# A fused Fourier-mixing and squared-ReLU kernel: chunks of 512 pairs instead of 256, 512-wide first-layer matmuls, one square for two steps, DFT matmuls in runs of three

## The chip, the cores and the metric

The kernel runs on one core of one Trainium2 chip. The metric is the device time of one execution in microseconds (us), median of several. The profile's span, from the first to the last instruction, is about 1.8 us shorter than the time of the same execution. A run counts as *fast* here if it lies within 1.5% of the fastest of its kernel. Engines in the profile are PE (TensorE, matmul), PEld (its weight loads), DVE (VectorE), ACT (ScalarE), POOL (GpSimd) and SP (SyncE).

## The reference

```python
# x: (8, 3008, 256) * 0.1;  w_in: (256, 2048);  w_out: (2048, 256)
X = np.fft.fft(np.fft.fft(x, axis=1), axis=2).real      # per batch
h = np.maximum(X.reshape(24064, 256) @ w_in, 0.0)
out = (h * h) @ w_out
```

The kernel folds the DFT over the model dimension into the first-layer weights (matrices G1, G2, G3) and does the DFT over the sequence as matmuls with cosine and sine tables on half of the frequencies. Frequency k and its mirror S-k form a *pair*: 1505 pairs per batch, 12040 in all. The hidden layer is computed for a *chunk* of pairs at a time. For an f-block of 128 hidden features, G1*P + G2*Q gives one member of the pair, and adding G3*Q to the same PSUM tile turns it into the other member. Each is sent through ReLU (ACT), squared (DVE) and used as stationary weights of the second layer.

## The kernel before

The parts that the change and the argument touch (cuts marked `# ...`):

```python
CH = 256                      # pairs in a chunk: 47 chunks of 256 and one of 8
psx = ctx.enter_context(tc.tile_pool(name="psx", bufs=3, space=PSUM))   # first layer, tables
pso = ctx.enter_context(tc.tile_pool(name="pso", bufs=2, space=PSUM))   # second layer
psf = ctx.enter_context(tc.tile_pool(name="psf", bufs=3, space=PSUM))   # DFT

def x_front(c, fp):           # one step: two f-blocks of one chunk
    # ...
    xb = psx.tile([P, 2, CH], F32, name="xb", tag="x")
    for j in range(2):
        fs = slice((fp * 2 + j) * P, (fp * 2 + j + 1) * P)
        for sn, G in ((0, G1), (1, G2)):
            for (b, i, o, l) in segs:           # two segments where a batch ends in the chunk
                mm(xb[:, j, o : o + l], G[:, fs], PQ[b][sn][:, i : i + l], first, sn == 1)
    # ...
    act(r[:, 0, :, 0:n], xb[:, :, 0:n], AF.Relu)

def x_back(cur):
    # ... the G3 matmuls into the same xb
    act(r[:, 1, :, 0:n], xb[:, :, 0:n], AF.Relu)
    vt(h2[:, 0, :, 0:n], r[:, 0, :, 0:n], r[:, 0, :, 0:n], op=ALU.mult)
    rr = r[:, 1, :, n - 1 :: -1]                # the mirror member, read in reverse
    vt(h2[:, 1, :, 0:n], rr, rr, op=ALU.mult)

for si, (c, fp) in enumerate(steps):
    take = [mmq.pop(0) for _ in range(min(len(mmq), 8))]   # second-layer matmuls, chunk before
    cur = x_front(c, fp)
    posts = [f() for f in take[:4]]
    if prev is not None:
        x_back(prev)
    posts += [f() for f in take[4:]]
    # ... evictions and stores of finished output tiles
    # ... mm2_ops of the chunk before join mmq when its last step is squared
    for f in side.get(si, []):                  # the next batch's fold (DVE) and DFT (PE, one
        f()                                     # matmul at a time), tables, weight casts
```

For each engine this is the order of its instructions. The second layer's matmuls are called `po` in the profile, the first layer's `xb`, the DFT's `pf`; `h` is the squared tile, `r` the ReLU output.

## Time and profile before

| | before |
|---|---|
| time, median of 3 runs | 658.08 us (657.77 to 658.36) |
| PE busy, share of the span of 657.9 us in the profiled execution | 635.4 us, 97% |
| ACT, DVE busy | 519.3 us, 403.3 us |
| matmuls po / xb / pf | 3040 / 2640 / 240 |
| granted TensorE clock | 1.0 |

These are lines of the page of the kernel before: busy time of each engine, the granted clock of PE in 40 equal slices of the span (9 is 90% or more), and the chain of waits that ended last, by engine and by engine, tile and line.

```profile
PE 635.4 (97%) x5954; PEld 550.0 (84%) x5954; DVE 403.3 (61%) x1078; ACT 519.3 (79%) x934; POOL 50.9 (8%) x66
...
PEclk9999999999999999999999999999999999999999
...
PE 94%; DVE 3%; DMA 1%; POOL 1%; ACT 1%; issue 0%; POOLq 0%; DVEq 0%
PE po L74 50%; PE xb L74 37%; PE pf L74 6%; DMA wst<-in_moe_w_in_dram 1%; POOL x L102 0%; DVE h L546 0%; DVE h L544 0%; DVE wout L603 0%; DVE tm L250 0%; ACT r L532 0%; ACT win L294 0%; PE ps L74 0%; DVE tt L246 0%; DVE v L334 0%; DVE tt L185 0%
```

The chain is PE almost throughout, so time is lost or won on PE. "Busy" alone does not tell whether PE is at its peak, since matmuls overlap in the record (272 ns long on average, 109 ns from start to start).

The page's groups of instructions: line, engine, operation, out<-in with shapes, count | busy us, mean ns of one | idle time before them and what ended most of it.

```profile
L74 PE MATMUL po<-wout,h 128*128 128x256 f16 (+1 forms) x3040 | 452.8, 272 | 0.0
L74 PE MATMUL xb<-qt,G 128*128 128x256 f16 (+8 forms) x1760 | 332.3, 257 | 3.3 <-ACT r L532 2.6
...
L546 DVE TENSOR_TENSOR h<-r 128x512 f16<-128x512 f16 (+1 forms) x384 | 160.6, 418 | 239.8 <-ACT r L542 239.1
L532 ACT ACTIVATE r<-xb 128x512 f16<-128x512 f32 (+1 forms) x384 | 226.5, 590 | 98.0 <-PE xb L74 86.1
```

One step in the steady state, from the timeline of the kernel before (start us, duration us, engine, line, operation, count; in brackets idle time before it and who ended it):

```profile
310.18 0.27 PE L74 MATMUL xb<-pt,G 128*128 128x256 f16 x1
310.29 0.27 PE L74 MATMUL xb<-qt,G 128*128 128x256 f16 x1
310.40 0.27 PE L74 MATMUL xb<-pt,G 128*128 128x256 f16 x1
310.51 0.27 PE L74 MATMUL xb<-qt,G 128*128 128x256 f16 x1
...
310.62 0.60 PE L74 MATMUL po<-wout,h 128*128 128x256 f16 x4
...
311.05 0.38 PE L74 MATMUL xb<-qt,G 128*128 128x256 f16 x2
...
311.06 0.42 DVE L544 TENSOR_TENSOR h<-r 128x512 f16<-128x512 f16 x1
...
311.27 0.60 PE L74 MATMUL po<-wout,h 128*128 128x256 f16 x4
311.47 0.60 ACT L542 ACTIVATE r<-xb 128x512 f16<-128x512 f32 x1
...
311.71 0.32 PE L74 MATMUL pf<-sinT,w 127*127 127x376 f16 x1
```

The durations, 0.27 us for a 256-wide matmul, are not what one costs: the starts are 0.11 us apart. From here on a matmul's cost is the distance from its start to the next one's start, taken from the matmul records. In this trace the median is 109 ns for the 256-wide po and 215 to 216 for the 512-wide matmuls (pc, ps). The line through 109 and 215.5 is 0.416 ns for each column plus 2.5 ns for each matmul. Sums below take 0.4167 ns and 2.5 ns. The 256-wide xb are at 110.

### The profile page before, as it was taken

What the parts mean: (1) busy time and instruction counts of PE and PEld (TensorE: products, weight loads), DVE (VectorE), ACT (ScalarE), POOL (GpSimd) and SP (SyncE); (2) the same over time, 40 slices, a digit from 0 to 9 for tenths busy, and PEclk for the clock granted to TensorE, in tenths of its full rate; (3) what the DMA queues carried; (4) which work ended last, traced back from release to release, by engine and by line L of the source; (5) the groups of instructions that cost most, each with busy time, mean ns of one, the idle gap of its engine ahead of it and who ended that gap; (6) DMA issues with size and microseconds to landing.
All of it is one profiled execution on the core that took longest, in us unless ns stands there. A gap on an engine that the chain in (4) does not pass through costs nothing.

```text
span 657.9 us, 14937 instructions
## 1 busy us (share of the span) xinstructions
PE 635.4 (97%) x5954; PEld 550.0 (84%) x5954; DVE 403.3 (61%) x1078; ACT 519.3 (79%) x934; POOL 50.9 (8%) x66
## 2 busy tenths in 40 slices
PE   3779999999999999999999999999999999999998
PEld 1458889888788889888898887988899888998886
DVE  7899559779587554865568555455545555454451
ACT  5787777877778888887888787888788888888883
POOL 7203003113020000400000000000000000000000
PEclk9999999999999999999999999999999999999999
DMA  8947218276355111721111111111111111111111
GB/s 244 291 116 188 67 35 225 77 207 168 102 132 142 35 38 43 202 70 50 33 49 34 50 40 43 33 45 40 47 35 50 37 46 41 41 45 45 42 49 50
DMA packets 33772, 54.65 MB, mean 83 GB/s; under 512 B 4446, under 2 KB 28562, under 8 KB 33702
## 3 DMA queue, kind: packets, MB, share of 16 engines
q0 software_dynamic: 6256, 27.45, 16.1%
q1 hardware_dynamic: 27398, 26.22, 12.8%
q8 instruction: 46, 0.75, 0.5%
q14 instruction: 24, 0.20, 0.1%
q10 hardware_dynamic: 48, 0.02, 0.0%
HBM read 29.02 MB, written 24.64 MB: 82 GB/s over the span
## 4 chain that ended last, share of the span: by engine, by line
PE 94%; DVE 3%; DMA 1%; POOL 1%; ACT 1%; issue 0%; POOLq 0%; DVEq 0%
PE po L74 50%; PE xb L74 37%; PE pf L74 6%; DMA wst<-in_moe_w_in_dram 1%; POOL x L102 0%; DVE h L546 0%; DVE h L544 0%; DVE wout L603 0%; DVE tm L250 0%; ACT r L532 0%; ACT win L294 0%; PE ps L74 0%; DVE tt L246 0%; DVE v L334 0%; DVE tt L185 0%
## 5 line engine op out<-in xcount | busy, mean ns | idle before, releaser
L74 PE MATMUL po<-wout,h 128*128 128x256 f16 (+1 forms) x3040 | 452.8, 272 | 0.0
L74 PE MATMUL xb<-qt,G 128*128 128x256 f16 (+8 forms) x1760 | 332.3, 257 | 3.3 <-ACT r L532 2.6
L74 PEld LDWEIGHTS <-h 128*128 128x128 f16 (+1 forms) x3040 | 289.9, 97 | 33.5 <-issue 0.2
L546 DVE TENSOR_TENSOR h<-r 128x512 f16<-128x512 f16 (+1 forms) x384 | 160.6, 418 | 239.8 <-ACT r L542 239.1
L532 ACT ACTIVATE r<-xb 128x512 f16<-128x512 f32 (+1 forms) x384 | 226.5, 590 | 98.0 <-PE xb L74 86.1
L74 PEld LDWEIGHTS <-G 128*128 128x128 f16 x2640 | 237.8, 97 | 44.9 <-issue 10.2
L542 ACT ACTIVATE r<-xb 128x512 f16<-128x512 f32 (+1 forms) x384 | 226.2, 589 | 20.4 <-PE xb L74 2.3
L74 PE MATMUL xb<-pt,G 128*128 128x256 f16 (+8 forms) x880 | 187.8, 257 | 0.7 <-ACT G L304 0.3
L544 DVE TENSOR_TENSOR h<-r 128x512 f16<-128x512 f16 (+1 forms) x384 | 158.1, 412 | 0.0
L476 ACT ACTIVATE os<-po 128x512 f32<-128x512 f32 (+1 forms) x95 | 56.3, 593 | 4.0 <-PE po L74 4.0
L326 DVE TENSOR_TENSOR u<-x 127x765 f16<-127x765 f32 x32 | 29.0, 948 | 2.4 <-DMA x<-in_x_dram,idx 2.4
L74 PE MATMUL pf<-cosT,w 127*128 127x377 f16 (+1 forms) x96 | 28.9, 325 | 0.4 <-DVE cosT L281 0.4
L74 PE MATMUL pf<-sinT,w 127*127 127x377 f16 (+1 forms) x96 | 28.9, 325 | 0.0
L102 POOL DMA_INDIRECT x<-in_x_dram,idx x18 | 26.6, 1478 | 5.4 <-issue 5.1
L74 PEld LDWEIGHTS <-w 127*128 127x128 f16 (+1 forms) x192 | 22.5, 118 | 3.0 <-DVE w L339 0.2
L125 POOL DMA_DIRECT2D x<-in_x_dram x14 | 7.8, 560 | 217.0 <-DVE u L330 217.0
L339 DVE TENSOR_TENSOR w<-v 127x381 f16<-127x381 f16 x64 | 20.4, 351 | 0.0
L334 DVE TENSOR_TENSOR v<-u 127x768 f16<-127x768 f16 x32 | 16.8, 548 | 0.0
L74 PEld LDWEIGHTS <-ez 127*128 127x128 f16 (+1 forms) x42 | 4.4, 107 | 14.7 <-DVE ez L565 10.9
L381 ACT ACTIVATE as<-pf 128x377 f32<-128x377 f32 (+5 forms) x32 | 15.5, 486 | 1.4 <-PE pf L74 1.1
L74 PE MATMUL warm<-ez 128*128 128x512 f16 x18 | 5.8, 484 | 10.9 <-DVE ez L565 10.9
L417 DVE TENSOR_TENSOR pt<-pf,as 128x377 f16<-128x377 f32 (+1 forms) x16 | 8.8, 547 | 0.3
(94 smaller groups left out, 122.6 us busy)
## 6 DMA issues: line engine op xcount, KB each, us to landing
out_dram<-os SPq DMA_DIRECT2D x157, 128.0 KB
x<-in_x_dram POOLq DMA_DIRECT2D x14, 756.0 KB
wst<-in_moe_w_in_dram POOLq DMA_DIRECT2D x4, 512.0 KB, 8.9
wot<-in_moe_w_out_dram POOLq DMA_DIRECT2D x1, 2048.0 KB, 18.8
x<-in_x_dram SPq DMA_DIRECT2D x2, 756.0 KB
x<-in_x_dram,idx POOLq DMA_INDIRECT x18, 11.2
x<-in_x_dram POOLq DMA_DIRECT2D x14, 2.0 KB, 10.8
out_dram<-os SPq DMA_DIRECT2D x2, 108.0 KB
```

The lines of the kernel that those rows point to most:

```text
L74: nc.tensor.matmul(o, l, r, start=start, stop=stop, skip_group_check=True)
L102: nc.gpsimd.indirect_dma_start(out=x4[0:NP, 2 + s, q : q + rows, :].rearrange("p q d -> p (q d)"), out_offset=None, in_=bass.AP(tensor=x.t ...
L326: return lambda: vt(u[k, s, q0 : q0 + NQ // 2, 1:D], x4[k, s, q0 : q0 + NQ // 2, 1:D], x4[k, 3 - s, ::-1, :][:, q0 : q0 + NQ // 2, D - 1 : ...
L334: return lambda: vt(v[k, s, qs, :], u[k, 0, qs, :], u[k, 1, qs, :], op=ALU.subtract if s else ALU.add)
L339: return lambda: vt(w[k, i, q : q + 3, 0 : P - 1], v[k, s, q : q + 3, 1:P], v[k, s, q : q + 3, D - 1 : P : -1], op=ALU.add if i < 2 else A ...
L381: act(st["a"][0:m, :], st[0][0:m, :], AF.Copy, bias=0.0, scale=1.0) \
L417: vt(hi_, bp, a, op=ALU.subtract)
L476: act(os_[0:m], st["o"][0:m], AF.Copy, bias=0.0, scale=HS * HS)
L532: act(r[:, 0, :, 0:n], xb[:, :, 0:n], AF.Relu)
L542: act(r[:, 1, :, 0:n], xb[:, :, 0:n], AF.Relu)
L544: vt(h2[:, 0, :, 0:n], r[:, 0, :, 0:n], r[:, 0, :, 0:n], op=ALU.mult)
L546: vt(h2[:, 1, :, 0:n], rr, rr, op=ALU.mult)
```

## The change

Its intent: fewer and wider first-layer matmuls (with a chunk of 512 pairs one f-block fills the 128 x 512 PSUM tile that two f-blocks of 256 shared), half of the weight loads of that layer, far fewer DVE instructions, and no chunk of 8 pairs at the end. The first two chunks stay at 256 pairs with two f-blocks per step. The diff, cut to its core:

```diff
-    NF = NFC // 2
-    CH = 256
+    CH = 512
-    osp = ctx.enter_context(tc.tile_pool(name="osp", bufs=4))
-    psx = ctx.enter_context(tc.tile_pool(name="psx", bufs=3, space=PSUM))
+    osp = ctx.enter_context(tc.tile_pool(name="osp", bufs=3))
+    psx = ctx.enter_context(tc.tile_pool(name="psx", bufs=6, space=PSUM))
-    psf = ctx.enter_context(tc.tile_pool(name="psf", bufs=3, space=PSUM))
 ... (SBUF space found: win16, v and the table temporaries share buffers)
-    def dft_ops(blk, mms, m, fin):            # one matmul per call
+    def dft_ops(blk, mms, m, fin, run=3):     # three matmuls per call; PSUM from psx
 ...
+    sizes = [CH // 2, CH // 2]
+    while sum(sizes) < NPAIR:
+        sizes.append(min(CH, NPAIR - sum(sizes)))     # 256, 256, 22 x 512, 264
 ...
+        groups = [tiles[i : i + 2] for i in range(0, len(tiles), 2)]
+        if n > full:                                  # the last 8 pairs: both members
+            groups.insert(0, [(2, full, n - full)])   # in one 16-wide weight tile
 ...
-        act(r[:, 1, :, 0:n], xb[:, :, 0:n], AF.Relu)
+        act(r_of(c, u, 1)[:, :, ::-1], xb, AF.Relu)   # ACT writes in reverse
 ...
+    def x_square(cur):
+        if u % 2 == 0:
+            return
+        # one multiply for two steps: 2048 elements per partition
+        vt(h2, r, r, op=ALU.mult)
 ...
-    FOLD = {0: [(1, 0.35, 0.52)], ...
-    ST1 = {0: (0.55, 0.95), 1: (0.25, 0.85)}
+    FOLD = {0: [(1, 0.5, 0.66)], ...
+    ST1 = {0: (0.66, 0.98)}                           # others 0.38 to 0.86
 ...
-        take = [mmq.pop(0) for _ in range(min(len(mmq), 8))]
+        left = NFC // chunks[c][2] - u
+        take = [mmq.pop(0) for _ in range(-(-len(mmq) // left))]
```

More of the change, by code (lines that the diff above doesn't have):

```diff
@@ L134 @@
     idx2 = iota("idx2", [P, 1], [[0, 1]], NQ // 2 * (NP - 1), -NQ // 2, I32)
-    win16 = const.tile([P, 2, F], F16, name="win16")
     wout16 = const.tile([P, NFC, D], F16, name="wout16")
@@ L235, in nk @@
                 if h == 0:
-                    tb["t"] = tgp.tile([P, NQ, HG], F32, name="tt", tag=f"tt{blk}")
-                    tb["m"] = tgp.tile([P, NQ, HG], F32, name="tm", tag=f"tm{blk}")
+                    tb["t"] = tgp.tile([P, NQ, HG], F32, name="tt", tag="tt")
+                    tb["m"] = tgp.tile([P, NQ, HG], F32, name="tm", tag="tm")
                 vt(views()[1], nval[:, qs].unsqueeze(2).to_broadcast([P, hq, ng]), kb, op=ALU.mult)
@@ L290, with win16 @@
     G3 = const.tile([P, F], F16, name="G3")
+    winh = {}
+    def win16(c):
+        if c // 2 not in winh:
+            winh[c // 2] = bfp.tile([P, 2, 1024], F16, name="win16", tag="w")
+        return winh[c // 2][:, :, c % 2 * 512 : c % 2 * 512 + 512]
     def gcast(c, cp):
-        cs = slice(c * 512, (c + 1) * 512)
-        cp(win16[:, :, cs], wst[:, :, cs])
+        cp(win16(c), wst[:, :, c * 512 : (c + 1) * 512])
     def gmat(c):
@@ L299, in gmat @@
         for t in range(2):
-            mm(pc, cosD[:, t, :], win16[:, t, cs], t == 0, t == 1)
+            mm(pc, cosD[:, t, :], win16(c)[:, t, :], t == 0, t == 1)
         ps = psx.tile([P, 512], F32, name="ps", tag="x")
         for t in range(2):
-            mm(ps, sinD[:, t, :], win16[:, t, cs], t == 0, t == 1)
+            mm(ps, sinD[:, t, :], win16(c)[:, t, :], t == 0, t == 1)
         act(G1[:, cs], pc, AF.Copy, bias=0.0, scale=1.0 / HS)
@@ L319, in fold_ops @@
         u = uvp.tile([P, 2, NQ, D], F16, name="u", tag="u")
-        v = uvp.tile([P, 2, NQ, D], F16, name="v", tag="v")
+        vs = {}
         w = bfp.tile([P, 4, NQ, P], F16, name="w", tag="w")
@@ L333, in half, with f @@
             qs = slice(h * NQ // 2, (h + 1) * NQ // 2)
-            return lambda: vt(v[k, s, qs, :], u[k, 0, qs, :], u[k, 1, qs, :],
-                              op=ALU.subtract if s else ALU.add)
+            def f():
+                if h == 0:
+                    vs[s] = uvp.tile([P, NQ, D], F16, name="v", tag="v")
+                vt(vs[s][k, qs, :], u[k, 0, qs, :], u[k, 1, qs, :],
+                   op=ALU.subtract if s else ALU.add)
+            return f
         def feat(i, q):
             s = i % 2
-            return lambda: vt(w[k, i, q : q + 3, 0 : P - 1], v[k, s, q : q + 3, 1:P],
-                              v[k, s, q : q + 3, D - 1 : P : -1],
+            return lambda: vt(w[k, i, q : q + 3, 0 : P - 1], vs[s][k, q : q + 3, 1:P],
+                              vs[s][k, q : q + 3, D - 1 : P : -1],
                               op=ALU.add if i < 2 else ALU.subtract)
@@ L344, in f @@
             def f():
-                nc.vector.tensor_copy(w[k, s, :, P - 1], v[k, s, :, 0])
+                nc.vector.tensor_copy(w[k, s, :, P - 1], vs[s][k, :, 0])
                 if b in INL:
-                    nc.vector.tensor_copy(ez[k, s, :, P - 1], v[k, s, :, P])
+                    nc.vector.tensor_copy(ez[k, s, :, P - 1], vs[s][k, :, P])
                 else:
-                    nc.vector.tensor_copy(eall[k, s, :, b], v[k, s, :, P])
+                    nc.vector.tensor_copy(eall[k, s, :, b], vs[s][k, :, P])
             return f
@@ L370, in dft_ops, with some, stage1_ops @@
         ops = []
-        def one(par, i):
+        def some(par, lo, hi):
             def f():
-                if i == 0:
-                    st[par] = psf.tile([P, HE], F32, name="pf", tag="pf")[:, 0:n]
-                hi, wt, q, tab = mms(par)[i]
-                mm(st[par][0:hi, :], wt(q), tab[k, q, c0 : c0 + n], i == 0, i == len(mms(par)) - 1)
-                if i == len(mms(par)) - 1:
-                    if par == 0:
-                        st["a"] = asp.tile([P, HE], F32, name="as", tag="as")[:, 0:n]
-                        act(st["a"][0:m, :], st[0][0:m, :], AF.Copy, bias=0.0, scale=1.0) \
-                            if fin[0] is None else act(st["a"][0:m, :], st[0][0:m, :], AF.Copy,
-                                                       bias=0.0, scale=fin[0])
-                    else:
-                        fin[1](st["a"][0:m, :], st[1][0:m, :])
+                ms = mms(par)
+                if lo == 0:
+                    st[par] = psx.tile([P, 512], F32, name="pf", tag="x")[:, 0:n]
+                for i in range(lo, hi):
+                    rows, wt, q, tab = ms[i]
+                    mm(st[par][0:rows, :], wt(q), tab[k, q, c0 : c0 + n], i == 0,
+                       i == len(ms) - 1)
+                if hi < len(ms):
+                    return
+                if par == 0:
+                    st["a"] = asp.tile([P, HE], F32, name="as", tag="as")[:, 0:n]
+                    act(st["a"][0:m, :], st[0][0:m, :], AF.Copy, bias=0.0,
+                        scale=1.0 if fin[0] is None else fin[0])
+                else:
+                    fin[1](st["a"][0:m, :], st[1][0:m, :])
             return f
         for par in range(2):
-            ops += [one(par, i) for i in range(len(mms(par)))]
+            nm = len(mms(par))
+            ops += [some(par, i, min(i + run, nm)) for i in range(0, nm, run)]
         return ops
-    def stage1_ops(b, blk, inline_e=False):
+    def stage1_ops(b, blk, inline_e=False, run=3):
         def lists(sn):
@@ L422, in stage1_ops @@
             ops += dft_ops(blk, lists(sn), P - 1 if sn and not inline_e else P,
-                           (sgn[:, 0:1] if sn and inline_e else None, fin(sn)))
+                           (sgn[:, 0:1] if sn and inline_e else None, fin(sn)), run)
         return ops
@@ L452 @@
     NPAIR = B * NK
+    sizes = [CH // 2, CH // 2]
+    while sum(sizes) < NPAIR:
+        sizes.append(min(CH, NPAIR - sum(sizes)))
+    assert all(n <= CH // 2 or n == CH or n % P < P // 4 for n in sizes)
     chunks = []
-    for g in range(0, NPAIR, CH):
-        n = min(CH, NPAIR - g)
+    g = 0
+    for n in sizes:
         segs = []
@@ L462, with h2v @@
             o += l
-        chunks.append((g, n, segs))
+        chunks.append((g, n, CH // n, segs))
+        g += n
     h2t = {}
+    def h2v(c):
+        n = chunks[c][1]
+        return h2t[c][:, 0 : NFC * 2 * n].rearrange("p (f t) -> p f t", f=NFC)
     def mm2_ops(c):
-        g0, n, segs = chunks[c]
-        tiles = [(s, t0, min(P, n - t0)) for s in range(2) for t0 in range(0, n, P)]
+        g0, n, nf, segs = chunks[c]
+        full = n // P * P
+        tiles = [(s, t0, P) for s in range(2) for t0 in range(0, full, P)]
+        groups = [tiles[i : i + 2] for i in range(0, len(tiles), 2)]
+        if n > full:
+            groups.insert(0, [(2, full, n - full)])
@@ L470, in mm2_ops @@
         ops = []
         st = {}
-        def store(grp):
-            os_ = osp.tile([P, 2, D], F32, name="os", tag="os")
-            m = max(t[2] for t in grp)
-            act(os_[0:m], st["o"][0:m], AF.Copy, bias=0.0, scale=HS * HS)
-            for j, (s, t0, m) in enumerate(grp):
-                o = 0
-                base = g0 + n - t0 - m if s else g0 + t0
-                while o < m:
-                    b, i = divmod(base + o, NK)
-                    if i < NE:
-                        l = min(m - o, NE - i)
-                        kk = 2 * i
-                    else:
-                        l = min(m - o, NK - i)
-                        kk = 2 * (i - NE) + 1
-                    lo, hi = 0, l
-                    if s and kk == 0:
-                        lo = 1
-                    if s and kk + 2 * (l - 1) == M:
-                        hi = l - 1
-                    if hi > lo:
-                        if s:
-                            r0 = b * S + S - (kk + 2 * (hi - 1))
-                            p0 = m - (o + hi)
-                        else:
-                            r0 = b * S + kk + 2 * lo
-                            p0 = o + lo
-                        nl = hi - lo
-                        nc.sync.dma_start(out=out[r0 : r0 + 2 * nl - 1 : 2, :],
-                                          in_=os_[p0 : p0 + nl, j, :])
-                    o += l
@@ L505, in one, with rows_out @@
-        def one(ti, fc):
-            s, t0, m = tiles[ti]
+        def rows_out(s, t0, m, src):
+            base = g0 + n - t0 - m if s else g0 + t0
+            o = 0
+            while o < m:
+                b, i = divmod(base + o, NK)
+                if i < NE:
+                    l = min(m - o, NE - i)
+                    kk = 2 * i
+                else:
+                    l = min(m - o, NK - i)
+                    kk = 2 * (i - NE) + 1
+                lo, hi = 0, l
+                if s and kk == 0:
+                    lo = 1
+                if s and kk + 2 * (l - 1) == M:
+                    hi = l - 1
+                if hi > lo:
+                    if s:
+                        r0 = b * S + S - (kk + 2 * (hi - 1))
+                        p0 = m - (o + hi)
+                    else:
+                        r0 = b * S + kk + 2 * lo
+                        p0 = o + lo
+                    nl = hi - lo
+                    nc.sync.dma_start(out=out[r0 : r0 + 2 * nl - 1 : 2, :], in_=src(p0, nl))
+                o += l
@@ new lines, in store @@
+        def store(grp, po):
+            os_ = osp.tile([P, 2, D], F32, name="os", tag="os")
+            if grp[0][0] == 2:
+                _, t0, m = grp[0]
+                act(os_[0 : 2 * m, 0], po[0 : 2 * m, 0], AF.Copy, bias=0.0, scale=HS * HS)
+                rows_out(0, t0, m, lambda p0, nl: os_[p0 : p0 + nl, 0, :])
+                rows_out(1, t0, m, lambda p0, nl: os_[m + p0 : m + p0 + nl, 0, :])
+                return
+            act(os_, po, AF.Copy, bias=0.0, scale=HS * HS)
+            for j, (s, t0, m) in enumerate(grp):
+                rows_out(s, t0, m, lambda p0, nl, j=j: os_[p0 : p0 + nl, j, :])
@@ L508, in f, with one @@
+        def one(grp, j, fc):
+            s, t0, m = grp[j]
             def f():
-                if ti % 2 == 0 and fc == 0:
+                if j == 0 and fc == 0:
                     st["o"] = pso.tile([P, 2, D], F32, name="po", tag="po")
-                mm(st["o"][0:m, ti % 2, :], h2t[c][:, s, fc, t0 : t0 + m], wout16[:, fc, :],
-                   fc == 0 and ti % 2 == 0, fc == NFC - 1)
-                if fc == NFC - 1 and ti % 2 == 1:
-                    return lambda: store(tiles[ti - 1 : ti + 1])
@@ L515, in one @@
-            return f
-        return [one(ti, fc) for ti in range(len(tiles)) for fc in range(NFC)]
-    def x_front(c, fp):
-        g0, n, segs = chunks[c]
-        if fp == 0:
-            h2t[c] = h2p.tile([P, 2, NFC, CH], F16, name="h2", tag="h2")
-        xb = psx.tile([P, 2, CH], F32, name="xb", tag="x")
-        first = True
-        for j in range(2):
-            fs = slice((fp * 2 + j) * P, (fp * 2 + j + 1) * P)
+                o = n + n % P + t0 if s == 1 else t0
+                w = 2 * m if s == 2 else m
@@ new lines, in f, with r_of @@
+                mm(st["o"][0:w, j, :], h2v(c)[:, fc, o : o + w], wout16[:, fc, :],
+                   fc == 0 and j == 0, fc == NFC - 1)
+                if fc == NFC - 1 and j == len(grp) - 1:
+                    return lambda o=st["o"]: store(grp, o)
+            return f
+        for grp in groups:
+            ops += [one(grp, j, fc) for j in range(len(grp)) for fc in range(NFC)]
+        return ops
+    rt = {}
+    def r_of(c, u, s):
+        g0, n, nf, segs = chunks[c]
+        if u % 2 == 0 and s == 0:
+            t = rp.tile([P, 4 * CH], F16, name="r", tag="r")
+            rt[c, u // 2] = t[:, 0 : 4 * nf * n].rearrange("p (f s n) -> p f s n", f=2 * nf, s=2)
+        o = u % 2 * nf
+        return rt[c, u // 2][:, o : o + nf, s, :]
@@ L527, in x_front @@
+    def x_front(c, u):
+        g0, n, nf, segs = chunks[c]
+        xb = psx.tile([P, 512], F32, name="xb", tag="x")[:, 0 : nf * n] \
+            .rearrange("p (f n) -> p f n", f=nf)
+        for j in range(nf):
+            fs = slice((u * nf + j) * P, (u * nf + j + 1) * P)
             for sn, G in ((0, G1), (1, G2)):
                 for (b, i, o, l) in segs:
-                    mm(xb[:, j, o : o + l], G[:, fs], PQ[b][sn][:, i : i + l], first, sn == 1)
-                    first = False
-        r = rp.tile([P, 2, 2, CH], F16, name="r", tag="r")
@@ L532, in x_front @@
-        act(r[:, 0, :, 0:n], xb[:, :, 0:n], AF.Relu)
-        return (c, fp, xb, r)
+                    mm(xb[:, j, o : o + l], G[:, fs], PQ[b][sn][:, i : i + l],
+                       j == 0 and sn == 0 and o == 0, sn == 1)
+        act(r_of(c, u, 0), xb, AF.Relu)
+        return (c, u, xb)
     def x_back(cur):
-        c, fp, xb, r = cur
-        g0, n, segs = chunks[c]
-        for j in range(2):
-            fs = slice((fp * 2 + j) * P, (fp * 2 + j + 1) * P)
+        c, u, xb = cur
+        g0, n, nf, segs = chunks[c]
@@ L540, in x_back @@
+        for j in range(nf):
+            fs = slice((u * nf + j) * P, (u * nf + j + 1) * P)
             for (b, i, o, l) in segs:
                 mm(xb[:, j, o : o + l], G3[:, fs], PQ[b][1][:, i : i + l], False, True)
-        act(r[:, 1, :, 0:n], xb[:, :, 0:n], AF.Relu)
-        h2 = h2t[c][:, :, 2 * fp : 2 * fp + 2, :]
-        vt(h2[:, 0, :, 0:n], r[:, 0, :, 0:n], r[:, 0, :, 0:n], op=ALU.mult)
-        rr = r[:, 1, :, n - 1 :: -1]
-        vt(h2[:, 1, :, 0:n], rr, rr, op=ALU.mult)
+        act(r_of(c, u, 1)[:, :, ::-1], xb, AF.Relu)
@@ new lines, in x_square @@
+    def x_square(cur):
+        c, u, _ = cur
+        nf = chunks[c][2]
+        if u % 2 == 0:
+            return
+        if u == 1:
+            h2t[c] = h2p.tile([P, NFC * 2 * CH], F16, name="h2", tag="h2")
+        r = rt.pop((c, u // 2))
+        n = chunks[c][1]
+        h2 = h2v(c)[:, (u - 1) * nf : (u + 1) * nf]
+        if n % P == 0:
+            h2 = h2.rearrange("p f (s n) -> p f s n", s=2)
+            vt(h2, r, r, op=ALU.mult)
+            return
+        full = n // P * P
+        for s, i, l, o in ((0, 0, n, 0), (1, full, n - full, n), (1, 0, full, 2 * n - full)):
+            vt(h2[:, :, o : o + l], r[:, :, s, i : i + l], r[:, :, s, i : i + l], op=ALU.mult)
@@ L580 @@
     gcast(2, nc.vector.tensor_copy)
-    s1 = stage1_ops(0, 0, True)
+    s1 = stage1_ops(0, 0, True, 1)
     for i in (0, 1, 3, 2, *range(4, len(s1))):
@@ L585 @@
     gcast(3, nc.vector.tensor_copy)
-    steps = [(c, fp) for c in range(len(chunks)) for fp in range(NF)]
+    steps = [(c, u) for c, ch in enumerate(chunks) for u in range(NFC // ch[2])]
     first_step = {}
-    for si, (c, fp) in enumerate(steps):
-        first_step.setdefault(chunks[c][2][-1][0], si)
+    for si, (c, u) in enumerate(steps):
+        first_step.setdefault(chunks[c][3][-1][0], si)
     side = {}
@@ L611 @@
     spread(stage1_ops(0, 1, True), 11, 15)
-    FOLD = {0: [(1, 0.35, 0.52)], 1: [(2, 0.02, 0.2), (3, 0.38, 0.56), (4, 0.7, 0.85)],
+    FOLD = {0: [(1, 0.5, 0.66)], 1: [(2, 0.02, 0.2), (3, 0.38, 0.56), (4, 0.7, 0.85)],
             2: [(5, 0.1, 0.4)], 3: [(6, 0.1, 0.4)], 4: [(7, 0.1, 0.4)]}
-    ST1 = {0: (0.55, 0.95), 1: (0.25, 0.85)}
+    ST1 = {0: (0.66, 0.98)}
     EGRP = {1: [2, 3, 4], 4: [5, 6, 7]}
@@ L622 @@
         side.setdefault(at(0.0) + 1, []).append(lambda bb=b + 1: alloc_pq(bb))
-        lo, hi = ST1.get(b, (0.05, 0.85))
+        lo, hi = ST1.get(b, (0.38, 0.86))
         spread(stage1_ops(b + 1, 0, b + 1 in INL) + stage1_ops(b + 1, 1, b + 1 in INL), at(lo), at(hi))
@@ L628 @@
         elif b + 1 not in INL:
-            side.setdefault(at(0.3), []).append(lambda bb=b + 1: e_row(bb))
+            side.setdefault(at(0.4), []).append(lambda bb=b + 1: e_row(bb))
     prev = None
     mmq = []
-    for si, (c, fp) in enumerate(steps):
-        take = [mmq.pop(0) for _ in range(min(len(mmq), 8))]
-        cur = x_front(c, fp)
-        posts = [f() for f in take[:4]]
+    for si, (c, u) in enumerate(steps):
+        left = NFC // chunks[c][2] - u
+        take = [mmq.pop(0) for _ in range(-(-len(mmq) // left))]
+        cur = x_front(c, u)
+        h = len(take) // 2
+        posts = [f() for f in take[:h]]
         if prev is not None:
             x_back(prev)
-        posts += [f() for f in take[4:]]
+        posts += [f() for f in take[h:]]
         for p in posts:
@@ L642 @@
                 p()
-        if prev is not None and prev[1] == NF - 1:
-            mmq += mm2_ops(prev[0])
+        if prev is not None:
+            x_square(prev)
+            if prev[0] != c:
+                mmq += mm2_ops(prev[0])
         prev = cur
@@ L648 @@
     x_back(prev)
+    x_square(prev)
     mmq += mm2_ops(prev[0])
```

## The prediction

> **What bounds it now.** TensorE: the page has PE busy 635 of 658 us, and the chain of waits is 94% PE (po 50%, xb 37%, pf 6%). Busy is not peak, so I took start-to-start distances from the matmul records: 256-wide every 109 to 110 ns, 512-wide (pc, ps) 215 to 216, 377-wide pf 159 to 165, a 31-wide segment 26.[...] Weight loads are hidden. From the first xb (23.2 us) to the last matmul (654.5) the stream takes 631 us; columns plus 2.5 ns each come to 617. The other 14 us: 8.3 before 45 us (the ramp: xb waiting for ACT relu, ps for a PSUM buffer, pf for cosT), about 2 around the 3-column e matmuls (93 to 98 ns before and after each), 1 in the 8-pair last chunk, the rest under 1 ns per matmul. The granted clock is 1.0 throughout.
>
> **What the change does on PE.** The hidden layer's columns stay the same, so 512-wide saves only the fixed part.
> - xb matmuls 2640 to 1536 (seven batch boundaries still split): 1104 x 2.5 ns = 2.8 us.
> - Both 8-pair halves share one po tile: 16 fewer po matmuls, 1.75 us.
> - The 8-pair chunk merges into a 264-wide one: with its small stalls about 2 us.
> - e matmuls in runs of three: about 1 us. Six shared PSUM buffers in the ramp: 0.5 us.
> Sum about 8 us.
>
> **Elsewhere.** DVE: four squares (418 and 412 ns) become one of 2048 elements. From the 512-element square (418) and the 768-element f16 add (548) I estimate 0.51 ns per element, 1.2 us. DVE busy falls from 403 to about 310 us, nearly all off the critical path. ACT: the same 768 relus of about 0.59 us (the next starts 0.49 us later), half with a reversed write; the reversed table mirrors (376 elements, 0.60 us) show no penalty. ACT stays about 510 to 520 us.
>
> **New waits on PE**, about 2 to 3 us in sum: each chunk's first step has no second-layer work (0.65 us of PE work against two relus, 0.98), and the last square comes 1.2 us after its relu, so po number 15 and 16 may arrive early where DVE is folding; the first 512-chunk has only 64 po to spread against 32 relus; batch 1 must be ready at pair 1024, not 1280; the end waits for relu, squares and a full 128-row store.
>
> **Predicted:** 652.5 us, 8 in 10 between 647.5 and 657. Faster by over 2%: 0.06; within 2%: 0.90; slower by over 2%: 0.04. With no waits at all after 23 us it would be 639.
>
> **What would show it right.** po 3024 matmuls, xb 1536; 512-wide xb start to start 216 ns; PE over 93% of the chain; DVE near 310, ACT within 10 us of 519; PE's waits for DVE h and ACT r under 4 us after 50 us; the last matmul 5 to 6 us earlier, the ramp unchanged within 1.5 us.
>
> **What would make it wrong.** po waiting for the whole h2 tile rather than its own f-block: up to 2 us per chunk, some 45 us in all. Reversed ACT writes at half rate: ACT becomes the limit. Stalls of over 3 us in the first 80 us, where the second batch's fold and DFT are squeezed into fewer steps. On the other side: if the ramp's 8 us went away with the larger PSUM pool, 645.

The forecast's sum: 2.8 + 1.75 + 2 + 1 + 0.5 = 8.05 us. Its 2.5 ns for each matmul follow from the distances in the trace before (2 x 109 - 215.5). That weight loads are hidden can be read there too: the loads for po take 97 ns on average, the po start every 109 ns, and the page shows 0.0 us of idle time before them.

## The result

| | before | after |
|---|---|---|
| time, median of 4 runs | 658.22 us (657.77 to 658.58) | 654.47 us (653.67 to 654.90) |
| PE / ACT / DVE busy | 635.4 / 519.3 / 403.3 us | 629.8 / 511.7 / 355.5 us |
| matmuls po / xb / pf | 3040 / 2640 / 240 | 3024 / 1536 / 240 |
| mean granted clock of the profiled run | 1.000 | 0.997 |

The ratio of the two is 0.9945, 95% interval 0.9931 to 0.9959. (A ratio here comes from the fast runs of both kernels in the same rounds; it is not quite the ratio of the medians.) The interval is clear of 1.

The page after, the same parts as before:

```profile
PE 629.8 (97%) x4834; PEld 459.5 (70%) x4834; DVE 355.5 (55%) x518; ACT 511.7 (78%) x934; POOL 49.4 (8%) x66
...
PEclk9989999999999999999999999999999999999999
...
PE 92%; DVE 4%; DMA 1%; ACT 1%; issue 0%; POOL 0%; DVEq 0%; ACTq 0%; POOLq 0%
PE po L72 50%; PE xb L72 36%; PE pf L72 6%; DMA x<-in_x_dram,idx 1%; DVE h L599 1%; DVE u L329 1%; DVE wout L660 0%; DVE v L341 0%; ACT r L585 0%; ACT r L575 0%; DVE tm L235 0%; DVE qt L422 0%; ACT os L533 0%; DVE tt L182 0%; ACT G L308 0%
```

PE is still the chain. The third digit of the clock row is an 8 where all others are 9: a stretch of lower clock early in the span, which this trace of the kernel before does not have. (The kernel before is not immune: of its 33 runs beside the experiments below, three show a clock of 0.997, at 662.2 to 662.7 us instead of about 658.5. No trace of one was kept, so the place and the cost of the fall are unknown there.) The groups after:

```profile
L72 PE MATMUL po<-wout,h 128*128 128x256 f16 x3024 | 445.7, 273 | 3.5 <-DVE h L599 3.5
...
L599 DVE TENSOR_TENSOR h<-r 128x2048 f16<-128x2048 f16 x184 | 225.2, 1224 | 250.8 <-ACT r L585 250.8
L575 ACT ACTIVATE r<-xb 128x512 f16<-128x512 f32 (+1 forms) x384 | 227.8, 593 | 91.2 <-PE xb L72 88.6
L72 PE MATMUL xb<-qt,G 128*128 128x512 f16 (+16 forms) x1024 | 286.5, 323 | 3.8 <-ACT r L575 2.5
```

The square is now one instruction of 2048 elements, 184 times. A steady step after:

```profile
310.40 0.38 PE L72 MATMUL xb<-pt,G 128*128 128x512 f16 x1
310.62 0.38 PE L72 MATMUL xb<-qt,G 128*128 128x512 f16 x1
...
310.79 1.23 DVE L599 TENSOR_TENSOR h<-r 128x2048 f16<-128x2048 f16 x1 [1.82 <-ACT r L585]
310.83 0.60 PE L72 MATMUL po<-wout,h 128*128 128x256 f16 x4
311.03 0.60 ACT L575 ACTIVATE r<-xb 128x512 f16<-128x512 f32 x1 [0.27 <-PE xb L72]
...
311.27 0.38 PE L72 MATMUL xb<-qt,G 128*128 128x512 f16 x1
...
311.49 0.60 PE L72 MATMUL po<-wout,h 128*128 128x256 f16 x4
311.69 0.60 ACT L585 ACTIVATE r<-xb 128x512 f16<-128x512 f32 x1
```

A 512-wide xb is followed 0.22 us later by the next one, and four po take the same 0.44 us as before. No gap: the steady state is as tight as it was.

**Where the time went.** The table splits the stretch from the first xb to the last matmul. "Columns + 2.5 ns" is the sum over the matmuls of 0.4167 ns for each column plus 2.5 ns. The rest is the excess of the actual distances over that: in a row of its own if it is over 30 ns for one matmul (a wait or a slow clock), and under "small" if less.

| us, from the matmul records | before | after | difference |
|---|---|---|---|
| columns + 2.5 ns each | 617.13 | 612.62 | -4.51 |
| small excess | 3.77 | 1.59 | -2.18 |
| waits until 62 us (the ramp) | 8.36 | 10.51 | +2.15 |
| waits, 62 to 615 us | 1.89 | 1.61 | -0.28 |
| waits after 615 us | 0.09 | 0.48 | +0.39 |
| sum: first xb to last matmul | 631.24 | 626.80 | -4.44 |
| start of the last matmul to the end of the span | 3.48 | 4.10 | +0.62 |

The last two rows give -3.82 us, against -3.75 in the medians. The spans differ by 6.0 us (657.9 and 651.9), but 2.2 us of that is the start of the first xb, 23.2 us and 21.0 us. Up to there the loads are the same, and in the other traces it starts anywhere from 21.0 to 22.3 us; runs of the kernel before have spans of mostly 656.3 to 656.9. With the 634.7 us of its table such a span puts the first xb at about 21.9 us. So the late start belongs to that one profiled execution, and it is not credited to the change.

So the steady gain is 6.7 us (the first two rows), and nearly a third of it is given back at the start. This is the place, in the timeline after (weight loads and some other lines left out):

```profile
36.31 0.38 PE L72 MATMUL po<-wout,h 128*128 128x256 f16 x2
...
36.88 1.01 DVE L341 TENSOR_TENSOR v<-u 127x768 f16<-127x768 f16 x2
...
37.81 1.22 DVE L599 TENSOR_TENSOR h<-r 128x2048 f16<-128x2048 f16 x1
...
39.08 0.61 PE L72 MATMUL po<-wout,h 128*128 128x256 f16 x2 [2.39 <-DVE h L599]
...
39.48 0.63 PE L72 MATMUL xb<-qt,G 128*128 128x256 f16 x2
...
39.91 1.27 PE L72 MATMUL po<-wout,h 128*128 128x256 f16 x5
...
40.98 0.42 PE L72 MATMUL xb<-pt,G 128*128 128x256 f16 x1
41.19 0.42 PE L72 MATMUL xb<-qt,G 128*128 128x256 f16 x1
```

After two po at 36.31 the next one waits for a square (`h`) and starts at 39.08. DVE does it from 37.81 on, after other work, among it the fold's v. Then the matmuls are 0.21 us apart instead of 0.11, although they are the same 256 columns. The granted clock in the busy times by stretch shows why. The columns are the stretch, its length, busy time (and instructions) of PE, PEld, DVE, ACT and POOL, the granted clock, the DMA share and GB/s. The bounds are, to 0.05 us, those between which the trace's clock record says 0.5, 39.04 to 42.45 us, and the stretches of the same length beside it:

```profile
35.60:39.00 3.40, 1.09 (x10) 0.73 (x8) 3.37 (x7) 2.59 (x5) 0.00 (x0) 1.00 0.48 150
39.00:42.40 3.40, 3.32 (x16) 2.33 (x17) 2.96 (x12) 1.15 (x3) 0.00 (x0) 0.51 0.00 0
42.40:45.80 3.40, 3.40 (x30) 2.72 (x29) 2.14 (x8) 2.16 (x5) 0.00 (x0) 0.99 0.00 0
```

PE is busy for 1.09 of 3.40 us, and then the clock is half for 3.41 us.

### The profile page after: what moved, and what is told of

It is laid out like the page before. It is cut to its first block, busy times and chain, and to the rows that moved or that the text cites. A ratio compares the mean times of both kernels' runs of the same rounds, so it can differ in the third digit from the quotient of the medians.

```text
span 651.9 us, 11930 instructions
## 1 busy us (share of the span) xinstructions
PE 629.8 (97%) x4834; PEld 459.5 (70%) x4834; DVE 355.5 (55%) x518; ACT 511.7 (78%) x934; POOL 49.4 (8%) x66
## 4 chain that ended last, share of the span: by engine, by line
PE 92%; DVE 4%; DMA 1%; ACT 1%; issue 0%; POOL 0%; DVEq 0%; ACTq 0%; POOLq 0%
PE po L72 50%; PE xb L72 36%; PE pf L72 6%; DMA x<-in_x_dram,idx 1%; DVE h L599 1%; DVE u L329 1%; DVE wout L660 0%; DVE v L341 0%; ACT r L585 0%; ACT r L575 0%; DVE tm L235 0%; DVE qt L422 0%; ACT os L533 0%; DVE tt L182 0%; ACT G L308 0%
## 5 line engine op out<-in xcount | busy, mean ns | idle before, releaser
L72 PE MATMUL po<-wout,h 128*128 128x256 f16 x3024 | 445.7, 273 | 3.5 <-DVE h L599 3.5
L72 PEld LDWEIGHTS <-h 128*128 128x128 f16 x3024 | 286.0, 98 | 122.3 <-DVE h L599 4.4
L599 DVE TENSOR_TENSOR h<-r 128x2048 f16<-128x2048 f16 x184 | 225.2, 1224 | 250.8 <-ACT r L585 250.8
L72 PE MATMUL xb<-qt,G 128*128 128x512 f16 (+16 forms) x1024 | 286.5, 323 | 3.8 <-ACT r L575 2.5
L72 PEld LDWEIGHTS <-G 128*128 128x128 f16 x1536 | 144.5, 98 | 41.7 <-issue 7.4
L72 PE MATMUL xb<-pt,G 128*128 128x512 f16 (+16 forms) x512 | 146.8, 324 | 0.0
L533 ACT ACTIVATE os<-po 128x512 f32<-128x512 f32 x94 | 55.7, 592 | 6.3 <-PE po L72 6.2
L72 PE MATMUL pf<-sinT,w 127*127 127x377 f16 (+1 forms) x96 | 20.7, 323 | 0.0
L72 PE MATMUL pf<-cosT,w 127*128 127x377 f16 (+1 forms) x96 | 20.0, 323 | 0.1
L425 DVE TENSOR_TENSOR pt<-as,pf 128x377 f16<-128x377 f32 (+1 forms) x16 | 8.8, 549 | 8.6 <-PE pf L72 7.5
```

The lines of the kernel that those rows point to most:

```text
L72: nc.tensor.matmul(o, l, r, start=start, stop=stop, skip_group_check=True)
L425: vt(lo_, a, bp, op=ALU.add)
L533: act(os_, po, AF.Copy, bias=0.0, scale=HS * HS)
L599: vt(h2, r, r, op=ALU.mult)
```

## The experiments

The theory at this point (A): wide matmuls and the smaller tail give about 6.7 us; a late square in DVE's queue costs 2.4 us at 36 us and another 1.1 us near 56 us; and the idle stretch makes the clock fall, for another 1.6 us. The rivals (B): the gain comes from DVE's relief or from the larger PSUM pool rather than from the width; and the fall of the clock is a symptom that costs nothing. Twelve runs were made, the changed kernel once more and eleven variants, all with correct results. They ran in three groups of rounds on three chips: e_fill, e_unpair, e_256 and e_run1; then a_again, e_fo8, e_psx and e_best; then the rest. Ratios are against the kernel before in the same rounds. Where two times of different groups are compared, the traces' ledgers (the table above, made for each run) decide.

| run | time, median (range) us | ratio to before (95%) |
|---|---|---|
| a_again: the changed kernel | 654.42 (654.08 to 654.73) | 0.9933 (0.9920 to 0.9947) |
| e_fill | 652.51 (652.42 to 653.25) | 0.9903 (0.9883 to 0.9924) |
| e_unpair | 652.59 (652.19 to 654.03) | 0.9907 (0.9886 to 0.9929) |
| e_256 | 656.91 (656.11 to 657.34) | 0.9966 (0.9945 to 0.9987) |
| e_run1 | 655.15 (653.63 to 655.47) | 0.9938 (0.9917 to 0.9960) |
| e_fo8 | 652.79 (652.16 to 652.93) | 0.9907 (0.9893 to 0.9921) |
| e_psx | 653.58 (653.16 to 655.75) | 0.9925 (0.9909 to 0.9941) |
| e_best | 651.69 (651.32 to 652.55) | 0.9895 (0.9881 to 0.9909) |
| e_po16 | 655.00 (654.15 to 656.84) | 0.9935 (0.9911 to 0.9960) |
| e_tail | 652.12 (651.21 to 654.52) | 0.9902 (0.9877 to 0.9927) |
| e_best_fold | 654.04 (652.10 to 654.61) | 0.9918 (0.9895 to 0.9942) |
| e_best_trig | 651.52 (651.12 to 651.82) | 0.9884 (0.9856 to 0.9912) |

### The changed kernel once more

> The changed kernel as it is, on the same chip as the next three, so that they have a neighbour to be compared with. If the fall of the granted clock near 39 us depends on [...] that the kernel does not control, its runs fall in two groups, clock 1.0 at about 652.8 us and clock 0.997 at about 654.4; if it depends on the kernel alone, all runs have 0.997.

All five runs had a clock of 0.996 or 0.997, as all four of the first measurement had. Two groups within one kernel did not appear here, but did in others with the same ramp: e_run1 ran at 653.6 us twice with clock 1.0 and at 655.1 to 655.5 four times with 0.996 or 0.997; e_tail and e_po16 split three to three, and e_256 stayed at 0.999 or 1.0 in all six. So the fall does not depend on the kernel alone. All of these count as fast runs, and a comparison of a microsecond must look at the clock too.

### Fill the gap: is it the idle stretch that lowers the clock?

```diff
+        if si == 10:
+            fill = psx.tile([P, 512], F32, name="fill", tag="x")
+            for _ in range(10):
+                mm(fill, G1[:, 0:P], G1[:, 0:512], True, True)
```

> The changed kernel (654.5 us) with ten independent 512-wide matmuls (2.16 us of work, result unused) put ahead of the second-layer matmuls of step 10, just where PE waits 2.4 us for the last square of chunk 0 and where the granted clock then reads 0.5 for 3.4 us. Theory A (the idle stretch itself makes the clock fall, and the slow 3.4 us cost about 1.6 us): the clock record shows no 0.5 between 30 and 60 us, the matmuls after the wait are 109 ns apart again instead of 213, and the time falls by 1.6 us to about 652.9. Theory B (the clock falls for another reason, or the fall costs nothing because DVE is the limit there): the time stays within 0.5 us of 654.5, or rises by up to 2 us for the added work.

The timeline of this run at the same place:

```profile
36.68 2.32 PE L72 MATMUL fill<-G 128*128 128x512 f16 x10
...
38.17 1.22 DVE L599 TENSOR_TENSOR h<-r 128x2048 f16<-128x2048 f16 x1
...
38.83 0.38 PE L72 MATMUL po<-wout,h 128*128 128x256 f16 x2
...
39.45 0.39 PE L72 MATMUL po<-wout,h 128*128 128x256 f16 x2 [0.23 <-DVE h L599]
...
39.90 0.71 PE L72 MATMUL po<-wout,h 128*128 128x256 f16 x5
```

The square starts and ends as late as before, PE waits only 0.23 us, and the five po from 39.90 take 0.71 us instead of 1.27. The clock record has no 0.5 there, and no run has a clock under 0.999. With 2.16 us of useless matmuls the kernel was 1.9 us faster than a_again (652.51 and 654.42, other rounds on another chip). By the records, the waits until 62 us fall from 10.51 to 6.72 us; adding the 2.16 us of filler leaves 1.63 us, which is what the slow clock cost. Theory A, with the size it gave.

The slow stretch in the changed kernel's trace is 3.413 us long. PE was not idle all the time before it: the wait was 2.39 us, and PE was busy for 1.09 of the 3.40 us ahead. Nor does such a wait always lower the clock. e_tail (below) has the same ramp, and its trace has the same long wait (2.4 us in the list of waits, 2.55 us of excess by the records), but at this place its clock stays at 1.00:

```profile
34.40:37.90 3.50, 2.31 (x21) 1.72 (x18) 3.47 (x7) 2.64 (x6) 0.00 (x0) 1.00 0.87 201
37.90:41.30 3.40, 2.20 (x21) 1.98 (x22) 3.38 (x10) 2.50 (x5) 0.00 (x0) 1.00 0.19 69
```

Two more traces with a wait of 2.4 us for the same square differ in the same way: e_po16's clock is 0.997, e_run1's is 1.0. What decides between the two was not shown.

### One square for each step

```diff
-        if u % 2 == 0:
-            return
 ...
+        h2 = h2v(c)[:, u * nf : (u + 1) * nf]      # 1024 elements, after every step
```

> The changed kernel, but a square after every step (1024 elements) instead of one for two steps (2048). Theory A (DVE's busy time is off the critical path, and pairing only delays the last square of a chunk): DVE busy rises by about 25 us to 380, nothing changes after 60 us, the wait of second-layer matmuls for squares near 36 and 56 us falls from 3.5 us to under 2.5, and the time falls by 1 to 3 us to about 652.5. Theory B (the relief of DVE by pairing is part of what made the kernel faster): the time rises by 1 us or more.

DVE's busy time rose to 381.4 us and the kernel got faster by 1.8 us (652.59, against 654.42 for a_again in other rounds). Between 62 and 615 us the waits are 1.61 us, exactly as with pairs. So the relief of DVE bought nothing, and the rival that credits it is refuted. But the gain is nearly all clock, which did not fall in any run. Until 62 us the waits are 8.81 us, against 10.51 with the slow clock and 8.87 in e_tail's trace, which has the changed kernel's ramp at full clock. The po that waited 2.55 us for a paired square loses only 0.1 us now, so pairing did delay that square, as theory A says. The time goes to other waits instead: 1.5 us of an xb for a ReLU at 37 us, 1.0 us of po for a square near 56 us (1.2 with pairs), 0.9 us of a pf after it (0.2 with pairs). What single squares avoid is the one long wait (2.39 us in the changed kernel's trace) after which the clock fell.

### 256-wide matmuls, all else kept

```diff
-    sizes = [CH // 2, CH // 2]
-    while sum(sizes) < NPAIR:
-        sizes.append(min(CH, NPAIR - sum(sizes)))
+    sizes = [CH // 2] * 46
+    sizes.append(NPAIR - sum(sizes))
```

> The changed kernel with chunks of 256 pairs (46 of them and the 264 at the end), two f-blocks per step, so first-layer matmuls are 256 wide again; paired squares, runs of three, shared PSUM pool and the merged tail stay. Theory A (512-wide saves the fixed 2.5 to 3 ns of each matmul and nothing else): first-layer matmuls 2592 instead of 1536, PE stream 2.7 to 3.2 us longer, time about 657.5. Theory B (the width is not what gives the gain): time within 0.7 us of 654.5.

656.91 us, with a clock of 0.999 or 1.0 in all runs, so it must be compared with a version of the changed kernel at that clock, such as e_tail's trace. Its matmul stream is 3.45 us longer (628.53 and 625.08), its waits 0.39 us smaller, so 1056 more matmuls cost 3.85 us: 3.6 ns each. The width does give the gain, somewhat more than the 2.5 ns each that was predicted; the 256-wide xb come at a median of 110 ns rather than 109, the 512-wide at 216.

### The DFT matmuls one at a time

```diff
-    def dft_ops(blk, mms, m, fin, run=3):
+    def dft_ops(blk, mms, m, fin, run=1):
```

> The changed kernel with the DFT matmuls one at a time between the steps again. Theory A (runs matter only for the 24 three-column e matmuls, whose weight loads cost about 95 ns each before and after): those again lose about 95 ns on both sides each instead of once per run, time up by 0.5 to 1.5 us to about 655.5; the other pf matmuls stay at about 160 ns. Theory B (runs block first-layer work for 0.48 us at a time and cost more than they save): the time falls.

At a clock of 0.996 or 0.997 it takes 655.1 to 655.5 us against 654.1 to 654.7 for a_again. The records put 0.4 us of it at the 3-column matmuls (waits between 62 and 615 us 1.99 and not 1.61 us) and 0.4 us in the small excess. Runs of three save about 0.8 us, as theory A has it. In the traces before and after, PE lost 93 to 98 ns at the switch from 128-column to 3-column weights and again at the switch back, and nothing between matmuls of the same narrow run (159 ns for 377 columns in the trace after); that the weight loads cause this was not shown.

### Part of the fold behind the square

```diff
-    spread(fo, 7, 12)
+    spread(fo, 8, 12)
```

> The changed kernel with the second half of batch 0's fold started at step 8 instead of step 7, so that two of its DVE operations (1.0 us) stand behind the last square of chunk 0 and not ahead of it. Theory A (the wait near 36 us is the square standing in DVE's queue behind other work): the wait falls from 2.4 us to about 1.4, the clock stays 1.0 in most runs, and the time is about 652.5. Theory B (DVE as a whole is behind, so the wait only moves to the DFT matmuls that need that fold): the same sum of waits before 50 us, time within 0.5 us of the changed kernel with the same clock.

The wait of po falls from 2.57 us of excess (a_again) to 1.62, the clock stays at 0.999 or 1.0 in all runs, and the time is 652.79 us. Waits of 0.57 and 0.11 us appear at 42 us between pf. So the square did stand behind the fold, as theory A says, but theory B is right for most of what this was worth: until 62 us the waits are 8.61 us, only 0.26 less than in e_tail's trace at the same clock, because the wait moves on. The rest of the gain is the clock.

### Separate PSUM pools

```diff
-    psx = ctx.enter_context(tc.tile_pool(name="psx", bufs=6, space=PSUM))
+    psx = ctx.enter_context(tc.tile_pool(name="psx", bufs=3, space=PSUM))
+    psf = ctx.enter_context(tc.tile_pool(name="psf", bufs=3, space=PSUM))
```

> The changed kernel with the PSUM pools apart again: three buffers for the first layer and three for the DFT instead of six shared. Theory A (sharing matters in the ramp only): the waits of the table matmuls (pc to ps) of 0.5 to 0.7 us come back, but ACT is the limit there, so the time rises by no more than 0.5 us; no new wait after 60 us. Theory B (512-wide steps with runs of three need the larger pool): waits of first-layer matmuls for ACT in most steps, time up by over 3 us.

The waits of 0.69 and 0.55 us between pc and ps are back. Until 62 us the waits sum to 9.63 us, against 8.87 in e_tail's trace at the same clock: 0.8 us. After that the only new wait is one of 0.23 us at 158 us. Sharing the pool matters almost only in the ramp. Five of six runs had a clock of at least 0.999, one 0.996 (655.75 us); the one wait that was long with the shared pool is 0.35 us shorter here.

### Sixteen second-layer matmuls more

```diff
-            groups.insert(0, [(2, full, n - full)])
+            groups.insert(0, [(2, full, n - full), (3, full, n - full)])   # 8 wide each
```

> The changed kernel with the last eight pairs' two halves as two 8-wide weight tiles again[...] instead of one 16-wide tile: 3040 second-layer matmuls instead of 3024. Theory A (each matmul of 256 columns costs its 109 ns whatever the width of its weights): the last chunk's stream is 1.7 us longer, and since the tail is all TensorE the time rises by about 1.7 us less the 0.3 us by which PE now waits there for squares, so 1.4 to 1.7 us, to about 656.0. Theory B (narrow weights are cheap or hidden): under 0.7 us.

The stream is 628.59 us against 626.80 in the changed kernel's trace, both with the slow stretch: 1.79 us for 16 matmuls, or 112 ns each, although each uses only 8 columns of weights. (In the trace before, the 8-wide po are 109 ns apart, and the switch to them costs 94 ns; after, 94 ns to the 16-wide ones and 96 back.) The median (655.0) mixes three runs at clock 1.0 (654.2) with three at 0.997 (655.8 to 656.8). At 0.997 a_again is 654.4, so the step is 1.4 to 2.4 us in time. Theory A.

### The small group last

```diff
-            groups.insert(0, [(2, full, n - full)])
+            groups.append([(2, full, n - full)])
```

> The changed kernel with the 16-wide group last instead of first in the last chunk, nothing else. Theory A (the last eviction and store of 128 rows cost more than those of 16 rows): from the last matmul's start to the last instruction 3.4 us instead of 4.1, time down by 0.5 to 0.9 us against the changed kernel with the same clock. Theory B (the store's length does not depend on its rows): no change.

From the last matmul to the last instruction it takes 3.34 us instead of 4.10. The medians (652.12 and 654.42) exaggerate the gain, since half of the runs here escaped the slow clock; 0.76 us is the part of this edit. The last evictions, first in the changed kernel, then in e_best, which has the same edit:

```profile
648.15 0.60 ACT L533 ACTIVATE os<-po 128x512 f32<-128x512 f32 x1 [2.90 <-PE po L72]
```

```profile
646.44 0.37 ACT L529 ACTIVATE os<-po 16x256 f32<-16x256 f32 x1 [1.25 <-PE po L72]
```

The last eviction takes 0.37 us for 16 rows of 256 and 0.60 us for 128 rows of 512; from its end to the end of the span, where the store is, it is 2.6 us and 3.15 us.

### A version that beats both

```diff
+        one = c < 2            # single squares in the first two chunks
-    spread(fo, 7, 12)
+    spread(fo, 8, 12)
-            groups.insert(0, [(2, full, n - full)])
+            groups.append([(2, full, n - full)])
```

> An attempt to beat both: single squares in the first two chunks only, the fold shifted by one step as in the run before, and the 16-wide group last instead of first in the last chunk, so that the last store is 16 rows. Theory A: waits of second-layer matmuls for squares under 1.5 us before 60 us, clock 1.0, last instruction within 3.5 us of the last matmul instead of 4.1, time 650 to 651.5. Theory B (the ramp is limited by DVE and ACT work as a whole): no more than 0.5 us better than the run with all squares single (652.6).

651.69 us, ratio 0.9895: 1.1% faster than the kernel before and 2.7 us faster than the changed kernel of the same rounds. The clock was at least 0.999 in all runs. By the ledgers the 2.7 us are 1.6 of clock, 0.76 of tail and 0.36 of waits in the ramp (8.51 us until 62 us, 8.87 in e_tail's trace). The longest wait, 1.5 us at 37 us, is now that of an xb for a ReLU on ACT.

### Two more shifts in the ramp

```diff
-    FOLD = {0: [(1, 0.5, 0.66)], ...       ST1 = {0: (0.66, 0.98)}
+    FOLD = {0: [(1, 0.55, 0.7)], ...       ST1 = {0: (0.7, 0.98)}
```

> The best so far (651.7 us) with batch 1's fold started two steps later (0.55 to 0.70 of the batch, DFT from 0.70), so that its first four DVE operations of 0.95 us stand behind the last square of chunk 1. Theory A (the 1.0 us wait near 55 us is that square in DVE's queue): the wait goes, and the DFT still finds its operands: 0.7 to 1.4 us faster, about 650.6. Theory B (DVE is full there, so the DFT matmuls wait instead): the same time within 0.4 us, with waits of pf for w.

A miss: 654.04 us, slower than e_best (other rounds on another chip); at full clock two runs took 652.1 and 652.2. The square of chunk 1 is on time, but the first DFT matmuls of batch 1 then wait for the fold:

```profile
57.27 1.22 DVE L605 TENSOR_TENSOR h<-r 128x2048 f16<-128x2048 f16 x1
...
58.40 1.02 DVE L341 TENSOR_TENSOR v<-u 127x768 f16<-127x768 f16 x2
...
59.61 1.16 DVE L347 TENSOR_TENSOR w<-v 127x381 f16<-127x381 f16 x4
60.02 0.65 PE L72 MATMUL pf<-cosT,w 127*128 127x377 f16 x3 [2.09 <-DVE w L347]
```

The 1.0 us wait became one of 2.1 us, and in four of six runs the clock fell to 0.997. Theory B holds: the wait goes from the square to the DFT's operands.

The second one adds, to the same shift:

```diff
-    spread(tr1[5:], 8, 9)     spread(mi1, 9, 12)      spread(stage1_ops(0, 1, True), 11, 15)
+    spread(tr1[5:], 9, 10)    spread(mi1, 10, 13)     spread(stage1_ops(0, 1, True), 12, 15)
```

> The run before with the second half of the second table (two Sin activations of 0.7 us that wait for DVE), its mirrors and batch 0's second DFT block each one step later. Theory A (first-layer matmuls near 37 us wait for a relu that stands in ACT's queue behind those activations): that wait of 1.5 us falls under 0.7 and the time falls by another 0.5 to 1 us. Theory B (the work must be done before pair 512 in any case): the waits reappear before 53 us as waits of pf for the tables or of xb for qt, time within 0.4 us of the run before or slower.

The wait near 37 us falls from 1.5 to 0.6 us as theory A has it, and the time is 651.52 us, ratio 0.9884. The 2.25 us of excess near 56.6 us from the fold's shift is still in it. This version is level with e_best. Its clock was full in all four runs, but its trace has a stretch of 3.41 us at that wait with PE busy for only 1.67 us, and e_best_fold, with the same wait, fell in four of six; four runs may be luck. The last shift without the fold's was not run.

## Why the prediction was right or wrong

The time was right: 654.47 us lies in the range of 647.5 to 657, 2 us above the 652.5 of the centre, and "within 2%" was given 0.90. Point by point:

- **What bounds the kernel** (PE, at 0.4167 ns for each column plus 2.5 ns): right; the ledger closes to 0.1 us with it.
- **"1104 x 2.5 ns = 2.8 us"** for fewer xb: right in kind, too small. e_256 measured 3.6 ns each for 1056 of them, 3.85 us; the other 48 are the 8-column ones of the point after the next.
- **"16 fewer po matmuls, 1.75 us"**: right, 1.79 us in e_po16.
- **"The 8-pair chunk merges ...: about 2 us"**: too large. In the records the 48 xb of 8 columns were 26 ns each, 1.25 us, of which 8 more columns each keep 0.16, and the change added 0.39 us of waits after 615 us, mostly for squares. About 0.7 us is left.
- **"e matmuls in runs of three: about 1 us", "Six shared PSUM buffers: 0.5 us"**: 0.8 and 0.8 us.
- **"DVE busy falls ... to about 310 us"**: wrong, 355.5. The step that failed is the subtraction of durations from a busy time. The square of 2048 elements took 1224 ns, as estimated (1.2 us). But DVE instructions overlap in the record (the second square of a step starts 0.34 us after the first of 0.42 us), so the 1078 durations before sum to 461 us in a busy time of 403. The squares covered only 291 us of it, not the 319 us of their durations, and 19 us of that lay under other DVE work; now they cover 233 us, 6 of them under other work.
- **"nearly all off the critical path"**: right, e_unpair gives the busy time back and loses nothing.
- **ACT within 10 us of 519, no penalty for reversed writes**: right, 511.7 us, and 603 ns for 512 elements against 598 before; the writes in order take 602 ns beside them. (The reversed mirrors that the prediction leaned on took 592 to 596 ns for 376 elements in the trace before, two sines written in order there 541 ns for 376 and 522 for 378: not half the rate, but not proof of no penalty.)
- **"New waits on PE, about 2 to 3 us in sum"**: the places were right (the last square behind the fold; the end; the last store), the size was not. In the ramp alone 2.55 us of excess at 36.4 us, 1.22 us at 56.5 us, and 1.63 us that the prediction had no term for: the clock. "The ramp unchanged within 1.5 us" was wrong by that: it grew by 2.15 us net, after what the PSUM pool saved.
- **PE over 93% of the chain**: 92%, just missed. **Waits under 4 us after 50 us**: right, about 1.1 us for DVE's h and none of length for r. **The last matmul 5 to 6 us earlier**: 4.4 us, counted from the first xb.

The gains came out at 7.9 us in sum (3.85, 1.79, 0.7, 0.8 and 0.8) against the 8.05 predicted, partly by luck: the width gave 1 us more, the small chunk 1.3 us less. What put the time 2 us above the centre is the slow clock, 1.63 us. Without it the new waits come to about 2.5 us net (7.9 us less the 3.8 of the ledger, less 1.63), the size predicted. The changed kernel at full clock would take about 652.8 us (an estimate from these runs: 654.42 less 1.63), next to the 652.5 predicted.

What stays open: why the changed kernel fell into the slow clock in all nine runs and others with the same ramp less often (e_run1, e_tail and e_po16 in 10 of 18, e_256 in none of 6). In all, 19 of 33 runs with this ramp fell. What decides was not shown; what was measured is how long PE was busy in the emptiest 3.41 us between 25 and 66 us of each trace. In the changed kernel's it is 1.02 us. In those of e_fill, e_unpair, e_fo8 and e_best it is not below 1.6 us, and none of their 22 runs fell. In those of e_psx and e_best_fold it is 1.37 and 1.32 us, and one and four of their six runs fell. In that of the kernel before it is 1.95 us, and still three of its 33 runs had a clock of 0.997, so no limit follows from this.

## What to carry to other kernels

In this kernel, with PE busy for 97% of the span, wider matmuls saved only a few ns for each instruction (3.6 ns in e_256), so multiply such a figure by the count before hoping for more, and look for the gain in the instructions that vanish (1.79 us for 16 po in e_po16). An off-path engine's busy time cost nothing here (26 us more on DVE in e_unpair), but the place of one instruction in its queue stopped the critical engine: batching two small squares into one moved the first result to the end of the batch, and po waited 2.39 us for it. That wait cost more than its length, because the clock fell after it (3.41 us at half clock, 1.63 us lost); independent filler matmuls showed that it did, and even paid here (e_fill, 1.9 us).
